# The opening of an attention and mixture-of-experts kernel: scores after two heads' maxima instead of four

## Chip, cores and metric

The kernel runs on one core of a Trainium2 chip. The metric is the device time of one execution in microseconds (us); the time of a kernel is the median of its runs. Engines are TensorE (PE in the profile; PEld are its weight loads), VectorE (DVE), ScalarE (ACT), GpSimd (POOL) and SyncE (SP), which here only issues transfers. A name with a q (SPq, ACTq) is the engine's sequencer, where transfers are issued.

## What is computed

```python
# 8 batches x 8 heads, 576 positions, head dimension 64
scores = q @ k.T / 8;  cum = cumsum(max(s, 0))
scores = where(causal, -1e9, scores + minimum(cum_k - cum_q, 0))
attn = exp(scores - rowmax);  x = attn / attn.sum() @ v
# then, for the 4608 rows of x (512 wide): a group of 4, an expert of 4 in it,
# out = group weight * expert weight * relu(x @ w1) @ w2
```

The change touches the attention stage only, which fills the first 420 us or so.

## The kernel before

**Work on one head.** There are 64 heads in 32 pairs; heads 2p and 2p + 1 form pair p. For each head TensorE makes the scores twice. The first time (the "maxima", `rowmax`, tiles `pm`) the queries stand on the rows: six matmuls of 64 to 448 columns, in one fp32r term, and VectorE reduces each with the mask to a maximum per query (tile `mx`, result in `mc`). The maxima are transposed on TensorE (`pmt`), split on VectorE into a high and a low row (`th`, `tl`), and two small transfers put these rows into rows 66 and 67 of the operand tile `WA`. That is the shift. The second time (`scores`, tiles `ps`) the keys stand on the rows: twelve matmuls, six from `WA` (68 rows: head dimension, two rows of cumulative sums, two of shift) and six from `WB` (the low parts). ScalarE takes the exponential into `pt` or `pu`, GpSimd zeroes what lies above the diagonal (an affine select, the "mask"), and `av` multiplies with the values in `VT`: 14 matmul records on TensorE, seven in the program. Then the result is normalised, transposed to rows and stored, and every fourth pair the router takes over a batch.

**Operands of a pair.** `load_raw(p)` brings q and k of a pair into one of three tiles `r`. `split` makes the high part on ScalarE (`hl`) and the low part by a subtraction (VectorE for pair 0, GpSimd for the others; its queue is "G"). `load_a` and `load_b` move the parts with transfers into `WA` (four tiles) and `WB` (five); in the first four pairs `place` lets ScalarE write some of them directly. `cumh` holds the cumulative sums in SBUF, `cumd` a copy in DRAM. `ones(i)` sets the constant rows of a `WA` tile.

**Steps.** The main loop runs over steps. Step n makes the scores of head n, the AV matmuls of head n - 1 and the maxima of head n + 4 (`LEAD = 4`). Steps -4 to -1 only make the maxima of heads 0 to 3; so the scores of head 0 come after four heads' maxima. Within a step a string gives the order by hand: `A3` is the fourth maximum matmul, `B0` the first unit of scores, `C2` the third AV matmul; a lower- or upper-case letter alone takes one waiting piece of work from a queue, such as `a` (maximum on VectorE), `b` (exponential), `e` (mask), `v` (AV result), `T`, `t` and `D` (transpose, split and transfer of shift rows), `G` (a low part), `S` (a split), and `R` a step of the router. Every engine keeps that order: TensorE, VectorE, ScalarE and GpSimd through step 62, and SyncE through step 0; after that SyncE's order is chosen by the scheduler.

The router object is made before the first step; its constants are set on GpSimd, and `operands()` makes six more on VectorE, one piece at each `R`, in steps 2 and 3.

Of the kernel before, what the change touches and what calls it, by code (L numbers as in the profile page):

```python
# [8 lines left out]
F32 = mybir.dt.float32  # L9
# [105 lines left out]
def attention(tc, qk, v, s, wr, xs, st):  # L115
# [3 lines left out]
    with ExitStack() as ctx:  # L119
# [57 lines left out]

        def load_a(p, placed=False):
            w = WA[p % NA]
            hl = hls[p].bitcast(F32)  # L180
            for h in range(2):
                if h or not placed:
                    nc.sync.dma_start(w[0:64, :, h, QO:].bitcast(F32), hl[h * 64:h * 64 + 64, 0:2])
                n = 2 * p + h
                nc.sync.dma_start(w[64:66, KA, h, QO:].bitcast(F32), (cumh if p < 4 else cumd)[n:n + 1].bitcast(F32))

        def load_b(p, placed=False):
            w = WB[p % NBB].bitcast(F32)
            hl = hls.pop(p).bitcast(F32)
            for h in range(2):  # L190

                hr = slice(h * 64, h * 64 + 64)
                b = slice(1 if placed and h else 0, 2)
                if h or not placed:
                    nc.sync.dma_start(w[0:64, QA, h], hl[hr, 1])
                nc.sync.dma_start(w[64:128, b, h], hl[hr, 0::2][:, b])
# [4 lines left out]
        def rowmax(n):  # L201
# [11 lines left out]
            def item(j, q0, rows, w, c0, cw):  # L213

                if n < LEAD and (j + c0) % 2:
# [10 lines left out]
                def most():  # L226
# [4 lines left out]
                    if h and c0:  # L231
                        push("T", p, lambda: shift_rows(p))
# [5 lines left out]
        def shift_rows(p):  # L238
            need("a", 2 * p + 1)
            i = p % NA  # L240
            pt = small(f"pmt{p}")
            nc.tensor.transpose(pt[:10, :P], mc[p % 2], ident)
            push("t", p, lambda: shifts(p, i, pt))

        def shifts(p, i, pt):
            th = sm.tile([10, P], F32R, name=f"th{p}", tag="th", bufs=1)
            tl = sm.tile([10, P], F32R, name=f"tl{p}", tag="tl", bufs=1)
            nc.vector.tensor_scalar(out=th, in0=pt[:10, :P], scalar1=-1.0, scalar2=None, op0=ALU.mult)
            nc.vector.scalar_tensor_tensor(out=tl, in0=pt[:10, :P], scalar=-1.0, in1=th.bitcast(F32), op0=ALU.mult,
                                           op1=ALU.subtract)  # L250
# [5 lines left out]
            push("D", p, send)  # L256
# [222 lines left out]
        def ones(i):  # L479
            for a in (QA, KA):  # L480
                nc.gpsimd.memset(WA[i][64:66 if a == QA else 68, a].bitcast(F32).rearrange("p h q -> p (h q)"), 1.0)

        nc.vector.tensor_scalar(out=r1, in0=s0, scalar1=0.0, scalar2=8.0, op0=ALU.max, op1=ALU.mult)

# [3 lines left out]
        ones(0)  # L488
# [14 lines left out]
        ones(1)  # L503
        ones(2)
        place(0, 0)
        split(0, 0)
        split(0, 1)
        load_a(0, True)
        split(1, 0)
        split(1, 1)  # L510
        place(0, 1)
        place(0, 2)
        place(1, 0)
        load_a(1, True)
        load_b(0, True)
        rt = Router(tc, ac, late, end, small, ring, wr_f, wr_sb, xs, st)
        place(1, 1)
        place(1, 2)
        place(2, 0)
        split(2, 0)  # L520
        split(2, 1)
        place(2, 1)
        place(2, 2)
        ones(3)
        for t in VT:
            nc.gpsimd.memset(t[:, 0:NB, 2], 1.0)


        pre = {-2: [(load_a, 2, True)],
               -1: [(load_b, 1, True), (load_v, 0), (load_raw, 3), (load_raw, 4)],  # L530
               0: [(place, 3, 0), (split, 3, 0), (split, 3, 1), (load_a, 3, True), (place, 3, 1), (place, 3, 2), (load_v, 1)],
               1: [(split, 4, 0), (split, 4, 1), (load_b, 2, True), (load_raw, 5)]}
# [7 lines left out]
        FIRST = [o.split() for i, o in enumerate((  # L540
# [4 lines left out]
        LAST = FIRST  # L545
        ENDS = ["W O o K X L M Q".split(), []]
        ORDER0 = "B0 b e A0 a T t B1 b D A1 a B2 b e A2 a B3 b e e A3 a B4 b e A4 a A5 a".split()
        for step in range(-LEAD, NH + 5):
            m, a = step + LEAD, step - 1
            A = rowmax(m) if m < NH else []  # L550
            Bq, C = [], []
            if 0 <= step < NH:
                need("T", step // 2)
                need("t", step // 2)
                need("D", step // 2)
# [12 lines left out]
            if step >= 2 and step // 2 + 4 < NP:  # L568
                push("S", step // 2 + 4, lambda p=step // 2 + 4, part=step % 2: split(p, part, True))
            named = {"A": A, "B": Bq, "C": C}  # L570
            order = FIRST if step < 3 else ORDERS if step < NH - 1 else LAST if step < NH + 2 else ENDS
            for part in order[step % 2] if step > 0 else ORDER0:
                if part[0] in named:
# [9 lines left out]
            for f, *args in pre.get(step, ()):  # L583
                f(*args)
            if step == -1:
                nc.sync.dma_start(cumd, cumh.bitcast(F32))
                rt.queue.append(rt.operands())
# [6 lines left out]
            if step % 2 == 0 and 0 < step and step // 2 + 5 < NP:  # L594
                need("S", step // 2 + 3)
                need("G", step // 2 + 3)
                load_raw(step // 2 + 5)
            if step % 2 == 1 and 0 < step < NH:
                for f, lead in ((load_a, 4), (load_b, 3), (load_v, 1)):
                    if step // 2 + lead < NP and (f != load_v or step > 1):  # L600
                        need("S", step // 2 + lead)
                        if f == load_b:
                            need("G", step // 2 + lead)
# [1105 lines left out]
```

## Time and profile before

| | us |
|---|---|
| median of 3 runs | 877.28 (876.32 to 877.72) |
| profiled execution | 876.57 |
| its span, from the first to the last instruction | 874.8 |
| TensorE busy | 840.2 |
| VectorE, ScalarE, GpSimd busy | 718.9, 615.7, 603.2 |

The span is one execution seen by the profiler; its own time holds 1.77 us more. Busy times are sums over the span, and matmuls are pipelined, so that a busy TensorE is not one at its peak.

### The profile page before, as it was taken

The numbers are of one execution on the slowest core, as the hardware profiler recorded it, in microseconds if no ns is written. First come the engines' busy times: TensorE is split into PE (matmuls) and PEld (weight loads), VectorE is DVE, ScalarE is ACT, GpSimd is POOL, SyncE is SP. The second block draws the span as 40 slices with busy tenths as digits, with TensorE's granted clock in tenths as the row PEclk, the third lists the DMA queues.
The fourth block names the chain that finished last, engine by engine and source line by source line (L and its number), as shares of the span: only waits on it lengthen the run. The fifth ranks groups of instructions, "written<-read, shape, count | busy, mean of one in ns | idle before, by whom it ended". The sixth has DMA issues, their size and how long they took to land. (4 is left out here: it accounts for less than half of the span.)

```text
span 874.8 us, 17801 instructions
## 1 busy us (share of the span) xinstructions
PE 840.2 (96%) x5601; PEld 774.2 (89%) x5601; DVE 718.9 (82%) x1975; ACT 615.7 (70%) x1397; POOL 603.2 (69%) x746
## 2 busy tenths in 40 slices
PE   4999999999999999998799999999999999999997
PEld 2788888888888888886689999999999999999996
DVE  7567787787878788787468799999999999999972
ACT  5668777787868777776656656776677767777760
POOL 9767677676877768545657956776777777777660
PEclk9999999999999999999899999999999999999999
DMA  6999898897979898723546655555656565666620
GB/s 189 256 246 253 233 243 225 218 244 195 251 208 241 224 238 209 180 63 121 173 137 216 219 175 202 203 175 187 228 202 195 182 220 198 235 211 223 218 94 26
DMA packets 81877, 174.06 MB, mean 199 GB/s; under 512 B 9676, under 2 KB 45132, under 8 KB 73584
## 3 DMA queue, kind: packets, MB, share of 16 engines
q1 hardware_dynamic: 71664, 152.93, 59.6%
q0 software_dynamic: 7488, 18.89, 5.8%
q10 hardware_dynamic: 2624, 1.03, 0.5%
q8 instruction: 46, 0.75, 0.3%
q14 instruction: 55, 0.45, 0.2%
HBM read 108.97 MB, written 19.69 MB: 147 GB/s over the span
## 5 line engine op out<-in xcount | busy, mean ns | idle before, releaser
L1016 POOL TENSOR_TENSOR wl<-raw,wh 128x512 fp32r<-128x512 f32 x163 | 209.7, 1299 | 82.4 <-ACT wh L1013 58.6
L1013 ACT CAST wh<-raw 128x512 fp32r<-128x512 f32 x256 | 153.9, 616 | 1.8 <-issue 1.8
L228 DVE CUSTOM_DVE_ANT_0 mx<-pm,mask 128x192 bf16<-128x192 f32 (+4 forms) x320 | 127.2, 418 | 31.4 <-PE pm L220 28.7
L1133 PE MATMUL ph<-xh,wh 128*128 128x256 f32 (+13 forms) x512 | 140.3, 300 | 1.8 <-DVE hl L1140 1.8
L220 PE MATMUL pm<-WA 66*128 66x288 f32 (+4 forms) x384 | 123.8, 355 | 15.3 <-DMA WA<-ch 9.5
L276 PE MATMUL ps<-WA 68*128 68x320 f32 (+4 forms) x384 | 135.9, 358 | 2.0 <-DMA WA<-tl 1.9
L1133 PE MATMUL ph<-xl,wh 128*128 128x256 f32 (+13 forms) x512 | 137.8, 301 | 0.0
L316 PE MATMUL po<-pt,VT 128*128 128x256 f32 (+3 forms) x512 | 119.4, 352 | 1.3 <-issue 1.0
L1212 PE MATMUL py<-hh,wh 128*128 128x256 f32 (+13 forms) x448 | 112.9, 302 | 0.0
L1212 PE MATMUL py<-hl,wh 128*128 128x256 f32 (+13 forms) x448 | 112.4, 301 | 0.0
L1139 ACT ACTIVATE hh<-ph 128x256 fp32r<-128x256 f32 (+13 forms) x128 | 53.3, 418 | 83.8 <-PE ph L1133 82.9
L278 PE MATMUL ps<-WB 128*128 128x320 f32 (+4 forms) x384 | 110.7, 301 | 0.0
L1265 DVE STREAM_TRANSPOSE yr<-yT 32x384 f32<-32x384 f32 (+1 forms) x208 | 104.6, 503 | 4.5 <-ACT yT L1209 0.4
L316 PE MATMUL po<-pu,VT 128*128 128x320 f32 (+1 forms) x384 | 105.5, 383 | 1.3 <-POOL pu L295 1.3
L1103 DVE STREAM_TRANSPOSE xt<-xg 32x256 f32<-32x256 f32 (+1 forms) x208 | 102.4, 492 | 2.7
L316 PEld LDWEIGHTS po<-pt,VT 128*128 128x128 f32 x512 | 88.2, 192 | 13.9 <-issue 1.5
L1133 PEld LDWEIGHTS ph<-xh,wh 128*128 128x128 f32 x512 | 95.9, 190 | 2.1 <-DVE hl L1140 1.9
L1133 PEld LDWEIGHTS ph<-xl,wh 128*128 128x128 f32 x512 | 95.2, 190 | 0.2
L162 POOL TENSOR_TENSOR WB<-r,hl 64x576 fp32r<-64x576 f32 x62 | 88.0, 1420 | 6.1 <-DMA WB<-hl 1.8
L1133 PE MATMUL ph<-xh,wl 128*128 128x256 f32 (+13 forms) x512 | 92.0, 299 | 0.0
L220 PEld LDWEIGHTS pm<-WA 66*128 66x128 f32 (+1 forms) x384 | 69.2, 193 | 25.1 <-DVE mc L228 9.8
L380 POOL TENSOR_TENSOR xTl<-xT,xTh 128x512 fp32r<-128x512 f32 x30 | 38.2, 1272 | 76.0 <-ACT xTh L376 55.4
(249 smaller groups left out, 2007.3 us busy)
## 6 DMA issues: line engine op xcount, KB each, us to landing
raw<-in_w_dram SPq DMA_DIRECT2D x64, 1024.0 KB
r<-in_qk_dram SPq DMA_DIRECT2D x32, 576.0 KB
WA<-hl SPq DMA_DIRECT2D x60, 288.0 KB
WB<-hl SPq DMA_DIRECT2D x60, 288.0 KB
VT<-in_v_dram SPq DMA_DIRECT2D x32, 384.0 KB
WB<-hl SPq DMA_DIRECT2D x64, 144.0 KB
xs<-xr SPq DMA_DIRECT2D x15, 512.0 KB
WA<-cumd SPq DMA_DIRECT2D x56, 4.5 KB
```

What stands on the lines that cost most here:

```text
L162: (nc.vector if p < 1 else nc.gpsimd).tensor_tensor(out=hl[:, 2] if part else WB[p % NBB][0:64, KA, h], in0=r[hr, part], in1=hl[hr, part]. ...
L220: nc.tensor.matmul(ps[:rows, :cw], WA[i][0:66, QA, h, QO + q0:QO + q0 + rows], WA[i][0:66, KA, h, QO + c0:QO + c0 + cw], start=True, stop= ...
L228: nc.vector.tensor_tensor_reduce(out=tmp[:rows, :cw], in0=ps[:rows, :cw], in1=mk[:rows], scale=1.0, scalar=-3.0e38 if c0 == 0 else mo, op0 ...
L276: nc.tensor.matmul(ps[:rows, o:o + w], WA[i][0:68, KA, h, QO + k0:QO + k0 + rows], WA[i][0:68, QA, h, QO + q0:QO + q0 + w], start=True, st ...
L278: nc.tensor.matmul(ps[:rows, o:o + w], WB[p % NBB][:, KA, h, k0:k0 + rows], WB[p % NBB][:, QA, h, q0:q0 + w], start=False, stop=True)
L316: nc.tensor.matmul(po[0][:, qa - base:qb - base], VT[p % NVT].rearrange("p t a d -> p (t a d)")[:, (3 * t + 1 + h) * 64:][:, 0:P], x[:, c: ...
L1013: self.casts.append(nc.scalar.copy(h[:, j], raw[:, j]))
L1016: self.low = lows[self.u, i, j] = nc.gpsimd.tensor_tensor(out=l[:, j], in0=raw[:, j], in1=h[:, j].bitcast(F32), op=ALU.subtract)
L1103: V.transpose(dst[:, 0:n, :, j], src[:, 0:n, :, i])
L1133: self.product = nc.tensor.matmul(pss[f][:, :cap], w[f // 4][:, c, (f % 4) * P:(f % 4 + 1) * P], x[:, c, :cap], start=(c == 0 and w is sel ...
L1212: self.product = nc.tensor.matmul(pss[c][:, :cap], w[2 + f // 4][:, f % 4, c * P:(c + 1) * P], x[:, f, :cap], start=(f == 0 and w is self. ...
L1265: V.transpose(dst[:, 0:n, :, i], src[:, 0:n, :, j])
```

## The change

The steps start at -1. In step -1 the maxima of heads 0 and 1 are made (the new token `N` takes the next maximum matmul, of whatever head is next), and step 0 makes the scores of head 0. The lead grows from two heads back to four in steps 1 to 6, which have eight `N` each instead of six. Eight order strings (`OPEN`) give the order of steps -1 to 6, the transfers' issue on SyncE among it: places, splits, low parts, loads and `ones` are tokens in them. Pair 0 sends the shift rows of each head by itself, `th` from ScalarE's queue and `tl` from SyncE's. ScalarE places head 1 of pair 0 in `WA` (a transfer did it). All low parts are made on GpSimd. The router object is made at the end of step 4; four of the six operand operations on VectorE are replaced by two iotas, the other two move to GpSimd. From pair 4 on one transfer brings the cumulative sums of both heads. From step 7 on the order strings are as before; the low parts of a pair are made two steps later than before.

```diff
-        def split(p, part, later=False):
-            if part == 0:
+        def split(p, part):
+            if p not in hls:
                 hls[p] = raw.tile([P, 3, S], F32R, name=f"hl{p}", tag="hl", bufs=3)
...
-                (nc.vector if p < 1 else nc.gpsimd).tensor_tensor(
-                    out=hl[:, 2] if part else WB[p % NBB][0:64, KA, h], in0=r[hr, part],
-                    in1=hl[hr, part].bitcast(F32), op=ALU.subtract)
+                nc.gpsimd.tensor_tensor(out=hl[:, 2] if part else WB[p % NBB][0:64, KA, h], in0=r[hr, part],
+                                        in1=hl[hr, part].bitcast(F32), op=ALU.subtract)
             for h in range(1 if part else 2):
-                if later:
-                    push("G", p, lambda h=h: low(h))
-                else:
-                    low(h)
+                push("G", p, lambda h=h: low(h))
...
             nc.scalar.copy(*((WA[p][0:64, :, 0, QO:], raws[p][0:64]) if part == 0 else
+                             (WA[p][0:64, :, 1, QO:], raws[p][64:128]) if part == 3 else
                              (WB[p][0:64, QA, 0], raws[p][0:64, 1]) if part == 1 else
...
-                if n < LEAD and (j + c0) % 2:
+                if n < 2 and (j + c0) % 2:
                     ps = ps_s.tile([P, 512], F32, name=f"pm{n}_{j}_{c0}", tag="ps")
...
-                    if h and c0:
-                        push("T", p, lambda: shift_rows(p))
+                    if c0 and (h or p == 0):
+                        push("T", p - (1 - h) / 2, lambda: shift_rows(p, h))
...
                 for r, t in ((66, th), (67, tl)):
-                    nc.scalar.dma_start(WA[i][r:r + 1, QA].bitcast(F32).rearrange("o h q -> o (h q)"), t.bitcast(F32))
+                    d = WA[i][r:r + 1, QA].bitcast(F32)
+                    e = nc.sync if r == 67 and p == 0 else nc.scalar
+                    e.dma_start((d if p else d[:, h:h + 1]).rearrange("o h q -> o (h q)"), t[:n].bitcast(F32))
...
+        ones(0, nc.vector)
         nc.vector.tensor_scalar(out=r1, in0=s0, scalar1=0.0, scalar2=8.0, op0=ALU.max, op1=ALU.mult)
...
+        OPEN = [o.split() for o in (
+            "c0 p00 p03 s01 G s00 c1 G G b00 c2 s11 s10 h1 p01 p10 w0 "
+            "N N N N N N N tt a v0 p02 t D N N N N b01 s21 s20 N G",
+            "N tt a t D r3 B0 b B1 b N a e h2 p11 B2 b N a e p12 B3 b e N a G B4 p20 b e N a G N a",
+            "B0 b N a C0 B1 b N a e C1 v v b10 b11 B2 b N a C2 r4 B3 b e N a C3 w1 o3 N a e B4 N b N tt a t D e C4 C5 "
+            "N a C6 v v v1 G c3 cd",
+            "C0 N a s31 C1 v v N a C2 B0 b s30 N a B1 b e C3 N a p30 B2 b e h3 N a C4 C5 B3 b N a e C6 v v e N a B4 b "
+            "N a p21 p22 b20 b21 r5",
+            "C0 B2 N a B0 N tt v e C1 B1 a t B3 v D N a Y b N a v a e b C2 b N a s41 e C3 N a e b e C4 v s40 N a Z B4 a "
+            "G N a C5 b C6 a p31 p32 a4 v2",
+            "B0 v b a N B2 v C0 e G a N a B3 C1 N a B1 N a C2 b e G C3 v N a s51 C4 B4 b v e a N a N tt a W e t C5 e D C6 b "
+            "N a s50 b30 b31 r6 a5 rt",
...
-        for step in range(-LEAD, NH + 5):
+        for step in range(-1, NH + 5):
             m, a = step + LEAD, step - 1
-            A = rowmax(m) if m < NH else []
+            A = rowmax(m) if len(OPEN) - 2 < step and m < NH else []
...
-            if step == 0:
+            if step == len(OPEN) - 2:
                 manual.close()
                 manual.enter_context(tc.manual_schedule(engines={ENG.PE, ENG.DVE, ENG.Activation, ENG.Pool}))
...
-        n1 = iota("n1", [[S, B], [P, NB]], base=1, cm=1, dt=I32)
-        self.part = ac.tile([P, 2, B, NB], F32, name="part")
-        ni = ac.tile([P, B, NB], I32, name="ni")
-        self.n1, self.ni, self.uf, self.onesf = n1, ni, uf, onesf
+        self.part = (iota("part0", [[S // 64, B], [P // 64, NB]]), iota("part1", [[0, B], [0, NB]], base=1, cm=1))
+        nc.gpsimd.tensor_copy(self.ub, uf)
+        nc.gpsimd.memset(self.ob, 1.0)
```

In the strings, `c` loads cumulative sums, `p` places (pair, part), `s` splits, `b` loads `WB` (pair, head), `h` loads head 1 of a pair into `WA`, `a` with a digit both heads, `r` a raw tile, `v` with a digit a tile of values, `w` and `o` set constants, `tt` makes the transpose of the maxima at once, `rt` the router object and `cd` writes `cumd`.

## Rows read from the trace of the kernel before

**Rows 1.** The page: busy time of each engine, share of the span, instructions.
```profile
PE 840.2 (96%) x5601; PEld 774.2 (89%) x5601; DVE 718.9 (82%) x1975; ACT 615.7 (70%) x1397; POOL 603.2 (69%) x746
```
**Rows 2.** Windows: stretch, length, busy PE, PEld, DVE, ACT, POOL; clock, DMA share, GB/s.
```profile
22.69:28.42 5.73, 5.53 (x22) 4.83 (x23) 2.82 (x13) 2.49 (x6) 3.36 (x8) 1.00 0.93 309
28.42:33.07 4.65, 4.65 (x15) 4.00 (x16) 1.35 (x8) 4.45 (x10) 3.23 (x3) 1.00 0.73 221
33.07:35.87 2.80, 2.80 (x20) 2.41 (x18) 1.62 (x6) 1.14 (x2) 2.66 (x7) 1.00 0.92 255
35.87:43.91 8.04, 7.34 (x40) 5.40 (x38) 7.37 (x21) 6.20 (x15) 6.19 (x8) 1.00 1.00 240
43.91:51.75 7.84, 5.78 (x29) 4.93 (x27) 5.76 (x18) 3.87 (x9) 4.42 (x7) 0.78 0.88 241
51.75:57.55 5.80, 5.80 (x37) 5.11 (x36) 3.88 (x13) 4.18 (x11) 4.44 (x6) 1.00 1.06 263
57.55:62.69 5.14, 5.14 (x37) 4.65 (x35) 4.08 (x18) 4.54 (x13) 2.57 (x5) 1.00 0.91 258
62.69:68.46 5.77, 5.77 (x38) 5.09 (x36) 3.88 (x13) 4.63 (x12) 5.57 (x9) 1.00 0.94 210
...
46.38:51.75 5.37, 5.37 (x26) 4.74 (x26) 3.33 (x14) 2.86 (x7) 2.27 (x4) 0.68 0.95 271
```
**Rows 3.** Timeline of the start: start us, length, engine, line, operation [idle before].
```profile
3.84 0.48 DVE L483 TENSOR_SCALAR cl<-cl 64x576 f32<-64x576 f32 x1 [3.84 <-DMA cl<-in_s_dram]
7.48 0.77 SPq L185 DMA_DIRECT2D WA<-ch  x1
9.45 0.95 PE L220 MATMUL pm<-WA 66*128 66x288 f32 x3 [9.45 <-DMA WA<-ch]
9.93 0.76 DVE L162 TENSOR_TENSOR hl<-r,hl 128x576 fp32r<-128x576 f32 x1
10.60 0.45 DVE L228 CUSTOM_DVE_ANT_0 mx<-pm,mask 128x288 bf16<-128x288 f32 x1
12.75 0.51 DVE L228 CUSTOM_DVE_ANT_0 mx<-pm,mask,mc 128x288 bf16<-128x288 f32 x1
15.91 0.38 PE L242 MATMUL pmt<-ident,mc 128*10 128x128 f32 x1 [0.21 <-DVE mc L228]
16.64 0.28 DVE L249 SCALAR_TENSOR_TENSOR tl<-pmt,th 10x128 fp32r<-10x128 f32 x1
16.64 1.62 ACTq L254 DMA_DIRECT2D WA<-th  x1
18.35 0.74 ACTq L254 DMA_DIRECT2D WA<-tl  x1
22.72 0.55 PE L276 MATMUL ps<-WA 68*128 68x256 f32 x1 [1.88 <-DMA WA<-tl]
```
**Rows 4.** Timeline: first and last of the router's six operations, then TensorE's wait.
```profile
37.63 1.42 DVE L699 CAST ub<-uf 128x128 bf16<-128x128 f32 x1
...
44.47 1.43 DVE L707 CAST part<-ni 128x40 f32<-128x40 int32 x1
...
46.38 0.36 PE L220 MATMUL pm<-WA 66*128 66x192 f32 x1 [2.06 <-DVE mc L228]
```
**Rows 5.** Timeline: ScalarE, GpSimd and a SyncE issue; last, a window of GpSimd's constants.
```profile
6.62 1.15 ACT L174 CAST WA<-r 64x1152 fp32r<-64x1152 f32 x1 [4.04 <-DMA r<-in_qk_dram]
7.68 2.39 ACT L158 CAST hl<-r 128x576 fp32r<-128x576 f32 x4
11.47 2.88 POOL L162 TENSOR_TENSOR WB<-r,hl 64x576 fp32r<-64x576 f32 x2
12.54 0.67 SPq L196 DMA_DIRECT2D WB<-hl  x1
...
15.78:17.60 1.82, 1.75 (x13) 1.00 0.40 108
```
**Rows 6.** Windows of steps 4 to 6, masks on GpSimd alone: length, busy, count.
```profile
51.75:68.46 16.71, 4.50 (x12) 1.00 0.97 243
```

More of the change, by code (lines that the diff above doesn't have):

```diff
@@ L176, in place, with load_h @@
                              (WB[p][64:128, KA, 1], raws[p][64:128, 0])))
-        def load_a(p, placed=False):
-            w = WA[p % NA]
-            hl = hls[p].bitcast(F32)
[L181 to L196, printed above, removed]
+        def load_h(p, h):
+            nc.sync.dma_start(WA[p % NA][0:64, :, h, QO:].bitcast(F32), hls[p].bitcast(F32)[h * 64:h * 64 + 64, 0:2])
@@ new lines, in load_c, with load_a, load_b @@
+        def load_c(p):
+            if p < 4:
+                for h in range(2):
+                    n = 2 * p + h
+                    nc.sync.dma_start(WA[p][64:66, KA, h, QO:].bitcast(F32), cumh[n:n + 1].bitcast(F32))
+            else:
+                nc.sync.dma_start(WA[p % NA][64:66, KA, :, QO:].bitcast(F32), cumd[2 * p:2 * p + 2].rearrange("h a s -> a h s"))
+        def load_a(p):
+            load_h(p, 0)
+            load_h(p, 1)
+            load_c(p)
+        def load_b(p, h, placed=False):
+            need("G", p)
+            w = WB[p % NBB].bitcast(F32)
+            hl = hls[p].bitcast(F32)
+            hr = slice(h * 64, h * 64 + 64)
+            b = slice(1 if placed and h else 0, 2)
+            if h or not placed:
+                nc.sync.dma_start(w[0:64, QA, h], hl[hr, 1])
+            nc.sync.dma_start(w[64:128, b, h], hl[hr, 0::2][:, b])
@@ L502, in attention, with router, most, turn @@
         make_identity(nc, ident)
-        ones(1)
         ones(2)
[L505 to L532, printed above, removed]
+        route_by = []
+        def router():
+            route_by.append(Router(tc, ac, late, end, small, ring, wr_f, wr_sb, xs, st))
+            route_by[0].queue.append(route_by[0].operands())
+        maxima, begun = [], [0]
+        def most():
+            if not maxima:
+                maxima.extend(rowmax(begun[0]))
+                begun[0] += 1
+            maxima.pop(0)()
+        def turn():
+            while not fifo["T"]:
+                pop("a")
+            pop("T")
+        acts = {"N": most, "tt": turn, "rt": router, "cd": lambda: nc.sync.dma_start(cumd, cumh.bitcast(F32))}
+        for n in range(10):
+            acts.update({f"o{n}": lambda n=n: ones(n), f"w{n}": lambda n=n: nc.gpsimd.memset(VT[n][:, 0:NB, 2], 1.0),
+                         f"r{n}": lambda n=n: load_raw(n), f"v{n}": lambda n=n: load_v(n), f"a{n}": lambda n=n: load_a(n),
+                         f"h{n}": lambda n=n: load_h(n, 1), f"c{n}": lambda n=n: load_c(n)})
+            for i in range(4):
+                acts.update({f"s{n}{i}": lambda n=n, i=i: split(n, i), f"p{n}{i}": lambda n=n, i=i: place(n, i),
+                             f"b{n}{i}": lambda n=n, i=i: load_b(n, i, n < 4)})
         vals, sums, pts = {}, {}, {}
@@ L539, in attention @@
             "e C4 v A1 Z B4 a R A5 C5 b C6 t a a"))]
[L540 removed]
+        LAST = [o.split() for o in (
             "B4 b e A1 a R B0 b e B1 b C0 A0 a R J T t C1 v v D A2 a R W C2 B2 b e O o Q A3 a R B3 b e e A4 a "
@@ L567, in attention @@
                 C = av(a, pts.pop(a), vals[p], sums[p])
-            if step >= 2 and step // 2 + 4 < NP:
-                push("S", step // 2 + 4, lambda p=step // 2 + 4, part=step % 2: split(p, part, True))
+            if step >= len(OPEN) - 2 and step // 2 + 4 < NP:
+                push("S", step // 2 + 4, lambda p=step // 2 + 4, part=step % 2: split(p, part))
             named = {"A": A, "B": Bq, "C": C}
-            order = FIRST if step < 3 else ORDERS if step < NH - 1 else LAST if step < NH + 2 else ENDS
-            for part in order[step % 2] if step > 0 else ORDER0:
-                if part[0] in named:
+            order = (OPEN[step + 1] if step + 1 < len(OPEN) else
+                     (ORDERS if step < NH - 1 else LAST if step < NH + 2 else ENDS)[step % 2])
+            for part in order:
+                if part in acts:
+                    acts[part]()
+                elif part[0] in named:
                     for f in named[part[0]][int(part[1]):int(part[1]) + 1]:
@@ L582, in attention @@
                     pop(part)
[L583 to L587, printed above, removed]
+            rt = route_by[0] if route_by else None
             if step == 62:
```

73 lines of the change are left out of this document (32 added, 41 removed), and 6 rows, old and new, of tables (FIRST, LAST, OPEN).

## Prediction

> **What bounds the kernel now.** I read the page first: TensorE is busy for 96% of the span, ahead of every other engine [rows 1]. A time saved anywhere is therefore kept only if TensorE's own line of work gets shorter or starts earlier. Then the windows, one for each step (the boundaries are the first score matmul of a step, or its first AV matmul where that comes first). Steps 4, 5 and 6 last 5.80, 5.14 and 5.77 us with TensorE busy throughout, 5.47 us in the mean of a pair (steps 4 and 5): the settled pace. Step 0 starts only at 22.69, and steps 1, 2 and 3 last 7.45, 8.04 and 7.84 us [rows 2]. So the opening loses time in two ways: a late start, and three long steps. From step 7 on, TensorE, VectorE and ScalarE execute the same instructions in the same order in both kernels (read off the order strings), so what is gained by then is kept.
>
> Then the timeline of the start. The first maximum matmul waits until 9.45 for the cumulative sums, which were issued at 7.48. VectorE is free for the first maximum at about 10.0 but still makes a low part from 9.93, and starts at 10.60; the last maximum of head 0 starts at 12.75 and takes 0.51. The transpose of the maxima runs at 15.91 because it waits for both heads; the low row `tl` is made at 16.64, issued only at 18.35, and TensorE waits for its landing until 22.72 [rows 3]. The scores are late by a transfer, not by the maxima of heads 2 and 3, which fill the wait.
>
> Third, the waits: the six operand operations of the router sit on VectorE between 37.63 and 45.9, in steps 2 and 3, and at 46.38 TensorE has waited 2.06 us for a maximum behind them [rows 4]. The stretch after it ran at a granted clock of 0.68, 26 matmuls in 5.37 us, 0.207 each, where step 4 has 37 in 5.80, 0.157 each [rows 2].
>
> **The change, part by part.** *Start of step 0.* Head 0's low part leaves VectorE, so its six maxima run from about 10.05 instead of 10.60 and end at 10.05 + 2.66 (12.75 + 0.51 - 10.60) = 12.7. From the transpose to the end of `tl` took 15.91 to 16.92, so `tl` is ready at 13.8 [rows 3]. On ScalarE the placing of two heads (1.15 each), four splits (2.39), one more place and two half ones (0.58 each) end at 6.62 + 7.0 = 13.6, in time for `th`. SyncE must first issue the loads put ahead of it: the first needs the low part that now runs on GpSimd (split done at 9.5, plus 1.44, so 11.0), then five issues of 0.67: 14.3 [rows 5]. The landing is the unknown: from issue to use, `ch` took 9.45 - 7.48 = 1.97 and `tl` 22.69 - 18.35 = 4.34 [rows 3]. The head's other transfers are just ahead of it on the queue, so I take 3.0, near the middle: step 0 starts at 17.3 (16.3 to 18.6), **-5.4**. The memsets of `ones(0)` on VectorE cost nothing, because VectorE waits for the data until 3.84; without that cover they would delay the cumulative sums by their length.
>
> [...]
>
> *Step 0* has the same matmuls as before: 5.73, no change. *Step 1* has two more maximum matmuls at the slow pace of the window from 28.42 (15 in 4.65, 0.31 each): +0.6. It also ends with a transpose that follows the maxima at once. Such a wait lies between 0.21 (the transpose at 15.91) and one maximum, 0.51 [rows 3]; 0.35 here, with one matmul between: **+0.95**.
>
> *Steps 2 to 6* each have two more maximum matmuls, 2 x 0.157 = 0.31, since two heads of lead (12 items) are made up in them and step 1. Their AV matmuls stand in more separate pieces; for that I take 0.3 a step (0 to 0.6), two matmuls' worth. Transposes that follow their maximum at once: 0.5 in steps 3 and 6, 0.35 in step 4.
>
> *Step 2* also needs the rows of heads 2 and 3, now made at the end of step 1. From the transpose, `tl` is ready after 1.0, `th` 0.28 earlier; both are issued by ScalarE, 0.74 each, then 1.97 to land: 0.73 + 0.74 + 1.97 = 3.4. TensorE has the transpose (0.38) and 15 matmuls of 0.157 ahead of these scores, 2.7: a wait of 0.7 (0 to 3.1, with 4.34 for the landing). ScalarE has its splits (2 x 0.60), a place (1.15) and two half places (1.16) on top of about 3.9 of a settled step (4.5 less a split) [rows 2, 5], 7.4 in all against 6.8, which I charge with 0.4. So step 2 is 5.47 + 0.31 + 0.3 + 0.7 + 0.4 = 7.2 where it was 8.04: **-0.85**. The router's operations are no longer on VectorE, so *step 3* is 5.47 + 0.31 + 0.3 + 0.5 = 6.6 where it was 7.84: **-1.25**. *Steps 4, 5, 6*: +0.95, +0.6, +1.1, **+2.65** together.
>
> Sum: -5.4 + 0.95 - 0.85 - 1.25 + 2.65 = **-3.9 us**. The profiled execution took 876.57 (span 874.8 and 1.77 around it), so 872.7; the median of the runs is 877.28, 0.71 above it, so the forecast is **873.4**.
>
> *Costed at nothing.* GpSimd: in steps 4 to 7 it has 13 low parts (1.44 each), 17 masks (4.50 / 12 = 0.375) and the router's constants (1.82 and about 0.6 more), 27.5 us [rows 5, 6] against 24.4 of step time, so it falls behind by 3. A mask is read a step later, which covers it; without that cover it costs 3. Transfers: raw tiles are loaded later, but one 288 KB transfer falls away and the windows moved 240 to 270 GB/s [rows 2]. The single `cumd` load for each later pair and the relaxed order of raw loads lie behind a busy TensorE.
>
> **The rivals.** *All of it hidden* (chance 0.20): no wait for rows in step 2, none at transposes, no cost of the pieces. Then -5.4 + 0.6 - 2.26 - 2.06 + 0.93 = -8.2: 869.1. For it: in the settled steps no transpose waits. Against: these orders put it right behind its maximum.
>
> *Late rows* (0.13): each shift row lands 4.34 after issue. Step 0 starts at 18.6 (+1.35) and step 2 waits 3.1 (+2.4): -0.15, 877.1. For it: the only landing of such a row that the trace shows; against: that window had the DMA share at 0.93 right after, and less is in flight now.
>
> *GpSimd becomes the bound* (0.08): masks come late in steps 5 to 8, 3 us back: -0.9, 876.4.
>
> *Slower: the slow pace lasts longer* (0.11). [...]
>
> **How the numbers follow.** Forecast 0.48 (its own range 871.0 to 875.5), hidden 0.20, late 0.13, GpSimd 0.08, slower 0.11. What can be told from no change is 0.2%, 1.75 us. Faster: 0.48 + 0.20 = 0.68; same: 0.13 + 0.08 = 0.21; slower 0.11. The range runs from 869.0, which cuts about half of the hidden case, to 878.5, which cuts the slower one.
>
> **What would show it.** First score matmul near 17.3, its wait put down to `tl`. No router operation on VectorE near 40, and no 2 us wait at a maximum. Step 2's first score waits under 1.5 us for `tl`. Steps 3 to 6 of 5.7 to 6.9 us with TensorE over 90% busy. The forecast is wrong if step 0 starts after 19, if the matmuls are still 0.25 apart after 32 us, or if ScalarE or GpSimd is what TensorE waits for in steps 2 to 6.

## The result and the profile after

The changed kernel takes 889.32 us, median of four runs (888.43 to 893.84), against 877.5 for the kernel before: a ratio of 1.0138, 95% interval 1.0094 to 1.0182. It is slower by 12 us, where 4 us less were forecast (873.4, range 869.0 to 878.5). The profiled execution is the longest of the four (893.84, span 892.1). It is 17.3 us longer than the profiled one before, and 12.9 of them are there when step 10 starts; that part, the opening, is what I read. Steps 10 to 19 take 59.6 us in both; the other 4.4 us come later in this one execution, and no run was made on them.

The page's first line answers [rows 1]:

```profile
PE 845.3 (95%) x5602; PEld 776.1 (87%) x5602; DVE 717.7 (80%) x1970; ACT 618.4 (69%) x1398; POOL 606.2 (68%) x750
```

Nothing is to be seen there: the same work, on the same engines. The windows of the steps (0, 1, 2, 3, 4, 5, 6, then 7 from its first AV matmul, then 8 and 9; columns as in [rows 2]) show the loss:

```profile
18.58:23.27 4.69, 4.69 (x17) 4.16 (x18) 1.42 (x7) 3.67 (x7) 1.06 (x4) 1.00 0.87 209
23.27:32.79 9.52, 9.21 (x36) 7.48 (x36) 4.73 (x22) 3.60 (x9) 8.02 (x11) 1.00 0.54 157
32.79:39.91 7.12, 6.02 (x36) 4.92 (x35) 2.91 (x13) 5.69 (x12) 0.72 (x3) 1.00 0.39 82
39.91:47.26 7.35, 6.33 (x36) 4.88 (x36) 5.65 (x24) 5.69 (x13) 4.75 (x8) 1.00 0.56 168
47.26:55.52 8.26, 6.29 (x37) 5.15 (x36) 5.21 (x20) 5.31 (x12) 6.65 (x20) 1.00 0.75 190
55.52:62.59 7.07, 6.64 (x38) 5.24 (x39) 4.17 (x19) 6.61 (x16) 5.46 (x10) 1.00 0.64 172
62.59:78.05 15.46, 6.54 (x37) 4.99 (x36) 6.43 (x20) 5.45 (x13) 7.50 (x10) 0.86 0.99 217
78.05:86.28 8.23, 8.23 (x37) 7.52 (x37) 3.52 (x14) 4.38 (x11) 4.27 (x8) 0.64 1.05 232
86.28:97.40 11.12, 11.12 (x71) 9.84 (x70) 8.10 (x29) 9.30 (x24) 9.71 (x13) 1.00 1.00 265
```

Step 6 starts at 62.59 where it was 62.69 before [rows 2], so by then the early start has been given back, but nothing is lost. Then step 6 takes 15.46 instead of 5.77. Look at the column before the last: the DMA share is 0.39 to 0.75 from step 1 to step 5, where the kernel before had 0.73 to 1.06, and from step 6 on it is 1.0. Two windows from the start, to step 6 and to step 10, first of the kernel before:

```profile
0.00:62.69 62.69, 46.38 (x211) 37.22 (x211) 42.95 (x149) 38.77 (x79) 48.31 (x97) 0.97 0.84 232
0.00:84.52 84.52, 68.21 (x349) 56.72 (x349) 58.91 (x209) 57.06 (x125) 64.55 (x121) 0.98 0.86 237
```

and of the changed one:

```profile
0.00:62.59 62.59, 44.82 (x209) 35.26 (x210) 36.00 (x138) 40.08 (x78) 41.23 (x93) 1.00 0.60 165
0.00:97.40 97.40, 70.71 (x349) 57.61 (x350) 54.05 (x201) 59.21 (x126) 62.70 (x122) 0.95 0.75 191
```

Length times share is the transfer time used: 72.7 us to step 10 before, 73.1 after. It is nearly the same transfer time (for somewhat fewer bytes: 237 GB/s over 84.52 us is 20.0 MB, 191 over 97.40 is 18.6), done by 84.52 in one and by 97.40 in the other: what differs is the time in which the DMA engines stood, 11.8 against 24.3 us. At step 6 the changed kernel has used 37.6 us of it, the kernel before 52.7.

Why they stood is in the timeline (raw loads, low parts on GpSimd, and what TensorE and ScalarE waited for):

```profile
14.54 0.87 SPq L260 DMA_DIRECT2D WA<-tl  x1
18.58 0.55 PE L282 MATMUL ps<-WA 68*128 68x256 f32 x1 [1.94 <-DMA WA<-tl]
24.84 1.41 POOL L162 TENSOR_TENSOR WB<-r,hl 64x576 fp32r<-64x576 f32 x1
26.28 0.33 SPq L151 DMA_DIRECT2D r<-in_qk_dram  x1
35.74 0.36 PE L282 MATMUL ps<-WA 68*128 68x256 f32 x1 [0.18 <-DMA WA<-tl]
40.14 2.89 POOL L162 TENSOR_TENSOR WB<-r,hl 64x576 fp32r<-64x576 f32 x2
43.06 0.34 SPq L151 DMA_DIRECT2D r<-in_qk_dram  x1
51.69 1.40 POOL L162 TENSOR_TENSOR WB<-r,hl 64x576 fp32r<-64x576 f32 x1
53.20 0.54 SPq L151 DMA_DIRECT2D r<-in_qk_dram  x1
62.39 1.40 POOL L162 TENSOR_TENSOR WB<-r,hl 64x576 fp32r<-64x576 f32 x1
63.81 0.35 SPq L151 DMA_DIRECT2D r<-in_qk_dram  x1
70.96 1.28 SPq L202 DMA_DIRECT2D VT<-in_v_dram  x2
73.71 0.67 ACT L158 CAST hl<-r 128x576 fp32r<-128x576 f32 x1 [4.35 <-DMA WB<-hl]
78.05 1.19 PE L322 MATMUL po<-pt,VT 128*128 128x256 f32 x2 [7.84 <-DMA VT<-in_v_dram]
```

Each raw load (pairs 4, 5, 6, 7) goes out 0.02 to 0.11 us after the end of the last low part of the pair three before, which held its tile. The low parts stand late in GpSimd's order, and SyncE keeps the written order through step 6, so all that is written behind a raw load waits with it, the values of pair 3 (70.96) too. In the kernel before the same four loads went out earlier (the first row is pair 3's load and pair 4's):

```profile
20.26 1.58 SPq L151 DMA_DIRECT2D r<-in_qk_dram  x2
...
30.19 0.33 SPq L151 DMA_DIRECT2D r<-in_qk_dram  x1
36.13 0.85 SPq L151 DMA_DIRECT2D r<-in_qk_dram  x1
47.83 0.94 SPq L151 DMA_DIRECT2D r<-in_qk_dram  x1
```

The four go out some 5, 13, 17 and 16 us later than there. In the stretch after the wait of 7.84 us (78.05 to 86.28) the granted clock reads 0.64, and 37 matmuls take 8.23, where 38 took 5.77 at 1.00 [rows 2].

### The profile page after: what moved, and what is told of

Same layout as the page of the kernel before. It is cut to its first block, busy times and chain, and to the rows that moved or that the text cites. A ratio compares the mean times of both kernels' runs of the same rounds, so it can differ in the third digit from the quotient of the medians.

```text
span 892.1 us, 17668 instructions
## 1 busy us (share of the span) xinstructions
PE 845.3 (95%) x5602; PEld 776.1 (87%) x5602; DVE 717.7 (80%) x1970; ACT 618.4 (69%) x1398; POOL 606.2 (68%) x750
## 3 DMA queue, kind: packets, MB, share of 16 engines
q10 hardware_dynamic: 2604, 1.02, 0.4%
## 5 line engine op out<-in xcount | busy, mean ns | idle before, releaser
L322 PE MATMUL po<-pt,VT 128*128 128x256 f32 (+3 forms) x512 | 121.8, 354 | 12.5 <-DMA VT<-in_v_dram 9.3
L162 POOL TENSOR_TENSOR WB<-r,hl 64x576 fp32r<-64x576 f32 x64 | 91.1, 1424 | 2.6
L301 POOL TENSOR_SCALAR_AFFINE_SELECT pt<-pt 128x128 f32<-128x128 f32 (+2 forms) x192 | 64.9, 350 | 38.3 <-ACT pt L292 34.7
```

The lines of the kernel that those rows point to most:

```text
L162: nc.gpsimd.tensor_tensor(out=hl[:, 2] if part else WB[p % NBB][0:64, KA, h], in0=r[hr, part], in1=hl[hr, part].bitcast(F32), op=ALU.subtract)
L322: nc.tensor.matmul(po[0][:, qa - base:qb - base], VT[p % NVT].rearrange("p t a d -> p (t a d)")[:, (3 * t + 1 + h) * 64:][:, 0:P], x[:, c: ...
```

## The experiments

Three theories come up first in the expectations; later ones are named where they come. **S**: the opening is bound by its transfers, and the change lets the DMA engines stand. **Q**: the value loads alone are late, because they are written last in SyncE's order. **R**: the engines' own order, the maxima caught up in steps 1 to 6 above all, is too long. All ratios are to the kernel before, run on the same chip.

**Values early.** The value loads of pairs 2 and 3 are written earlier in the strings.

```diff
-            "N a p21 p22 b20 b21 r5",
+            "N a p21 p22 b20 b21 v2 r5",
...
-            "N a s50 b30 b31 r6 a5 rt",
+            "N a s50 b30 b31 r6 a5 v3 rt",
...
```

> The changed kernel with two value loads moved forward in SyncE's hand-written order: the second pair's behind the WB loads of step 2, the third's to the end of step 4. Theory Q (the loads of values stand behind transfers that wait for later work, and TensorE waits 1.42 us and 7.84 us for them at 55.52 and 78.05): both waits go, and with them most of the 2.7 us of slow matmuls behind the second: 889.3 - 9.3 - 2.7, about 877. Theory S (transfers run dry from 30 to 50 us because raw tiles come free late, 110 GB/s where the kernel before moved about 228, and what is left over falls due at once from 60 us on): only the thing waited for changes, since the raw tile of pair 7 landed at 73.7 and holds ScalarE until then: 884 to 887.

889.27 us, 1.0148 (1.0128 to 1.0169). The wait for values is gone and nothing is gained:

```profile
73.28 0.67 ACT L158 CAST hl<-r 128x576 fp32r<-128x576 f32 x1 [3.94 <-DMA WB<-hl]
74.34 0.41 PE L282 MATMUL ps<-WA 68*128 68x320 f32 x1 [1.51 <-ACT pu L292]
83.93 0.67 ACT L158 CAST hl<-r 128x576 fp32r<-128x576 f32 x1 [4.15 <-DMA WB<-hl]
85.25 0.41 PE L282 MATMUL ps<-WA 68*128 68x320 f32 x1 [1.96 <-ACT pt L292]
```

ScalarE stops at a split until the loads that read the tile `hl` have run, and TensorE pays for it. Q falls: the longest wait named only the load that happened to come last. S had the change of waits right, but its time (884 to 887) is missed too.

**SyncE's order left to the scheduler** from step 1 on, as before the change.

```diff
-            if step == len(OPEN) - 2:
+            if step == 0:
                 manual.close()
```

> The changed kernel, but SyncE keeps the hand-written order only through step 0, as in the kernel before; from step 1 on the scheduler places its transfers. Theory Q: the scheduler issues the values as soon as their tile is free (it did so before, at 57.37), the two waits go: about 877. Theory S: raw tiles come free no earlier, 884 to 887.

886.73 us, 1.0135 (1.0101 to 1.0168), spread from 882.92 to 890.21. This is S's number. Its profiled execution is the fastest of the four, the change's the slowest: there step 10 starts at 89.14 instead of 97.40, but the time isn't told from the change's.

**Four raw tiles** (and four `WB` tiles instead of five), raw loads of pairs 4 to 7 one place earlier.

```diff
-        NA, NBB, NVT = 4, 5, 2
+        NA, NBB, NVT = 4, 4, 2
-            raws[p] = raw.tile([P, 2, S], F32, name=f"r{p}", tag="r", bufs=3)
+            raws[p] = raw.tile([P, 2, S], F32, name=f"r{p}", tag="r", bufs=4)
...
```

> The changed kernel with a fourth raw tile (paid for with one of the five WB tiles) and the raw loads of pairs 4 to 7 one place earlier in SyncE's order; the values stay last. Theory S: the DMA share between 30 and 50 us rises from 0.43 to over 0.6, the wait for values at step 7 falls from 7.84 to under 3: 881 to 884. Theory Q: the values still stand last behind the same waiting transfers, 7 us or more of waiting: 887 to 890.

888.2 us, 1.0134 (1.0111 to 1.0157). The time is Q's, the wait is S's: at step 7 TensorE waits 1.98 us for values instead of 7.84, but the DMA share from 30 to 50 us is 0.44 where S wanted over 0.6. Step 10 starts at 90.16 in the profile, and 3.9 us of that lead are given back right behind it (19.45 us to the transpose of step 12, 15.58 in the change). The kernel also has one `WB` tile less to the end, so the run doesn't show what a raw tile alone is worth.

**Low parts early.** The strings are rewritten so that a pair's low parts, splits, places and loads come about one step earlier; two of the eight show the kind of edit.

```diff
-            "N N N N N N N tt a v0 p02 t D N N N N b01 s21 s20 N G",
+            "N N N N N N N tt a v0 p02 t D N N N N b01 s21 s20 N G G G",
-            "N tt a t D r3 B0 b B1 b N a e h2 p11 B2 b N a e p12 B3 b e N a G B4 p20 b e N a G N a",
+            "N tt a t D r3 b10 b11 h2 B0 b B1 b N a e p11 B2 b N a e p12 B3 b e N a G B4 p20 b e N a G N a r4",
```

> The changed kernel with the opening's order strings rewritten so that the low parts, the splits, the places, the operand loads and the raw loads of each pair come about one step earlier than in the change (pair 1's low parts in step -1, pair 2's by step 1, pair 3's in step 2, and so on); nothing is added or removed. Theory S (the opening is bound by its transfers, and the change starves the DMA engines between 10 and 55 us because raw tiles come free late): the transfer time left idle before step 10 falls from 24.6 us to about 13, step 10 starts by 85 instead of 97.4, and the time is 873 to 879. Theory R (the loss is made on the engines' own order, in steps 1 to 4, whatever the transfers do): idle transfer time falls but step 10 stays after 92 and the time is 884 or more. If the order only moves the waits to VectorE or ScalarE, the waits at TensorE name those engines and the time is 880 to 886.

888.45 us, 1.0106 (1.0074 to 1.0139). Step 10 starts at 91.82, 5.6 earlier in the profile, and the DMA engines stand for 17 us (a share of 0.81 over 91.82) instead of 24. The direction is S's, the size isn't: S expected 873 to 879 and step 10 by 85. R's time (884 or more) came, and its mark for step 10 (after 92) is missed by 0.2.

**Fewer loads in the changed kernel.**

```diff
-            "G N a C5 b C6 a p31 p32 a4 v2",
+            "G N a C5 b C6 a p31 p32 a4",
-            "b a r8 b50 b51")]
+            "b a r8")]
-                if p - 1 < NP:
+                if p - 1 < NP and p - 1 != 6:
```

> The changed kernel without the loads of the low-part operands of pairs 5 and 6 and without the load of the values of pair 2: 2.16 MB less, all issued between steps 4 and 9; those heads compute with what the tiles held before. 2.16 MB at the 250 GB/s of the busy windows is 8.6 us of transfer work. Theory S: the debt of transfers at 60 to 90 us is smaller by about 8 us, so step 10 starts at 89 to 91 and the time is 880 to 883. Theory L (only the value loads that TensorE is seen to wait for matter; of these one is dropped, the wait of 1.42): 887 to 888. Theory R (engines' order): 888 to 889, with no change of step 10.

893.26 us, 1.0170 (1.0139 to 1.0201): no gain at all, against S, and above what any theory expected (880 to 889). Its timeline:

```profile
70.58 1.32 SPq L202 DMA_DIRECT2D VT<-in_v_dram  x2
77.06 1.19 PE L322 MATMUL po<-pt,VT 128*128 128x256 f32 x2 [7.54 <-DMA VT<-in_v_dram]
```

Most of what I left out goes out after the values of pair 3, which still leave at 70.58. So the bound of the changed kernel isn't the sum of the bytes; it is when they can be issued. S must be split: **C**, a chain (late low part, late raw tile, late loads behind it), and **T**, the transfers as a whole, once they are issued in time.

**Both links of the chain eased**: low parts early, SyncE's order left to the scheduler (the two edits above together).

> The kernel with the opening's low parts, splits, places and loads one step earlier, and besides SyncE's order left to the scheduler from step 1 on (as in the kernel before) instead of by hand through step 6. Theory C (a chain: a pair's low parts are made late, so its raw tile comes free late, so the next raw load, and in SyncE's hand order all that stands behind it, is issued late, and the transfer time lost so is never made up): both links of the chain are eased, step 10 starts by 87 to 89 instead of 91.8 and the time is 880 to 884. Theory T (the transfers bind whatever their order is, as soon as they are started early): transfer time idle before step 10 is no smaller than with the early low parts alone, step 10 at 91 to 92, time 887 to 889.

884.51 us, 1.0083 (1.0060 to 1.0106), step 10 at 90.26. That is 4.8 us below the change (in another round; the intervals of the two ratios just overlap). Both numbers lie between the theories, nearer to C's (880 to 884, step 10 by 87 to 89) than to T's. Two long waits are left at TensorE: 2.54 us for `tl` at 50.72, and 2.01 at 60.25 for an exponential, while ScalarE stands for 4.60 around its two issues of shift rows.

**The same with fewer loads** (2.16 MB, as above).

> The same as the run with early low parts and SyncE's order left to the scheduler, without the loads of the low-part operands of pairs 5 and 6 and of the values of pair 2 (2.16 MB; those heads compute with what the tiles held). In the changed kernel itself this omission gave nothing. Theory C with theory T behind it (once the chain is eased the transfers themselves bind, as they do in the kernel before, where the omission gave 4 us): 4 us or more below its twin with all loads, step 10 at 84 or before. If something else binds (ScalarE or VectorE in the opening's order): within 1 us of the twin.

881.62 us, 1.0048 (1.0033 to 1.0063), step 10 at 86.01: 2.9 us below its twin (the intervals just touch), 4.3 in the profile at step 10. The expectation wanted 4 us and step 10 at 84. Of the twin's two long waits the one for `tl` is gone and the other is 1.02. What gave nothing in the changed kernel gives about 3 us here, which fits T standing behind C.

**The router's part alone on the kernel before**, to see what the 2.06 us wait of [rows 4] was worth.

```diff
-        n1 = iota("n1", [[S, B], [P, NB]], base=1, cm=1, dt=I32)
-        self.part = ac.tile([P, 2, B, NB], F32, name="part")
...
+        self.part = (iota("part0", [[S // 64, B], [P // 64, NB]]), iota("part1", [[0, B], [0, NB]], base=1, cm=1))
+        nc.gpsimd.tensor_copy(self.ub, uf)
+        nc.gpsimd.memset(self.ob, 1.0)
```

> The kernel before with the router's part of the change alone: four operand operations of VectorE replaced by two iotas, two moved to GpSimd. If the 2.06 us wait at 46.38 and the slow stretch behind it come from these operations: 877.5 - 2.1 to 877.5 - 3.4, so 874.1 to 875.4. If TensorE would wait there for something else: 877.5.

877.49 us, 1.0008 (0.9988 to 1.0028): nothing that can be measured. The wait behind the router's operations is gone, and another stands ten us later:

```profile
52.02 0.75 ACTq L254 DMA_DIRECT2D WA<-th  x1
55.89 0.73 ACTq L254 DMA_DIRECT2D WA<-tl  x1
56.67 0.38 ACT L324 ACTIVATE sums<-po 64x256 f32<-64x256 f32 x1 [5.86 <-DMA WA<-th]
57.14 1.19 PE L316 MATMUL po<-pt,VT 128*128 128x256 f32 x2 [4.13 <-issue]
```

**The router's part and fewer loads.**

```diff
-                    if step // 2 + lead < NP and (f != load_v or step > 1):
+                    if step // 2 + lead < NP and (f != load_v or step > 3) and (f != load_b or step // 2 + lead not in (5, 6)):
```

> The kernel before with the router's part of the change alone (as in the run with the router alone), and without the loads of the low-part operands of pairs 5 and 6 and of the values of pair 2: those heads compute with what the tiles held. Theory S (the router's wait was hidden behind the transfers, which bind the opening of the kernel before as well): the wait of 4.13 for the values is gone and the missing gain shows: 872 to 875. If the transfers bind nothing there: 877 to 878, as with the router's part alone.

873.61 us, 0.9940 (0.9913 to 0.9966). The wait is gone and the gain shows: once the router's part is out of the way, the transfers bind the opening of the kernel before. (A load left out takes away its bytes and also every wait on it. The run further below that only moves the values of pairs 2 and 3 earlier gains nothing, which speaks for the bytes.) This kernel and the one with early low parts and fewer loads leave out the same loads, both have the router's part, and in neither does TensorE wait over 0.6 us for a transfer from step 1 to step 10; they differ by 8.0 us in the medians and by 6.4 in the profiles at step 10. There the difference ends: steps 10 to 19 take 59.56 and 59.72 us, though the later loads of cumulative sums and low parts aren't placed alike either. Steps 4, 5 and 6, first on the kernel before (this one), then on the changed one:

```profile
46.88:53.46 6.58, 6.58 (x40) 5.82 (x39) 4.43 (x16) 4.54 (x11) 5.35 (x9) 1.00 0.87 220
53.46:57.79 4.33, 4.33 (x32) 3.92 (x31) 3.53 (x14) 4.19 (x12) 2.55 (x4) 1.00 0.65 165
57.79:64.38 6.59, 6.59 (x41) 5.82 (x40) 4.43 (x16) 4.98 (x12) 5.59 (x9) 1.00 0.52 141
```

```profile
47.46:55.99 8.53, 7.22 (x41) 5.78 (x41) 5.53 (x22) 4.28 (x10) 8.04 (x22) 1.00 0.85 220
55.99:61.90 5.91, 5.48 (x34) 4.40 (x34) 3.76 (x16) 5.18 (x14) 5.25 (x8) 1.00 0.46 151
61.90:70.41 8.51, 7.43 (x42) 6.11 (x41) 5.62 (x20) 5.11 (x12) 4.12 (x7) 1.00 0.39 93
```

22.95 us against 17.50: 2.6 more of TensorE's own time (20.13 busy against 17.50) and 2.8 in which it stands. The start of step 0 is 2.1 us earlier, steps 0 to 9 are 8.5 longer, 5.45 of it here. This is R's part.

**Waits of the hand order.** On the kernel with both links eased, two transposes stand later and one exponential earlier.

```diff
-            "v2 C0 B2 N a B0 N tt v e C1 B1 a t B3 v D N a Y b N a v a e b C2 b N a s51 e G C3 N a e b e C4 v s50 N a Z B4 a "
+            "v2 C0 B2 N a B0 N v e C1 B1 tt a t B3 v D N a Y b N a v a e b C2 b N a s51 e G C3 N a e b e C4 v s50 N a Z B4 a "
...
-            "B0 v b a N B2 v C0 e G a N a B3 C1 N a B1 N a C2 b e G C3 v N a s61 C4 B4 b v e a N a N tt a W e t C5 e D C6 b "
+            "B0 v b a N B2 v C0 e G a N a B3 C1 N a B1 N a C2 b e G C3 v N a s61 C4 B4 b v e a N a N tt a W e t C5 e b D C6 "
...
-            "B0 v b a N N tt B2 v C0 a t e G a N a B3 D C1 N a B1 N a C2 b e G C3 v N a C4 B4 b v e a N a W e N C5 e C6 S "
+            "B0 v b a N N B2 v C0 tt a t e G a N a B3 D C1 N a B1 N a C2 b e G C3 v N a C4 B4 b v e a N a W e N C5 e C6 S "
```

> The kernel with early low parts and SyncE's order left to the scheduler, with three places of the hand order changed: in steps 3 and 6 the transpose of the maxima stands a few tokens later, so that TensorE needn't wait for VectorE's last maximum (0.79 at 42.3 and 1.03 at 68.2 us there), and at the end of step 4 ScalarE takes the last exponential before it issues the shift rows (TensorE waits 2.01 for that exponential at 60.25). Theory R (what is left of the loss once the transfers are eased is the opening's own order: the maxima caught up in steps 1 to 6 and the waits around them): the three waits go, step 7 starts 2.5 to 3.5 us earlier, 881 to 882. Theory T (the transfers bind there anyway): other waits, for operands, take their place and the time stays at 884 to 885.

884.55 us, 1.0093 (1.0066 to 1.0120). This is T's number. The three waits are gone and step 10 starts 1.1 us earlier in the profile, but the time is that of its twin: 2.12 us for `tl` at 50.71 stay, and waits of 0.45 to 0.70 for ScalarE's exponentials are new. With all loads in place, what is taken out of the order is not kept; R's waits aren't the bound by themselves. The same edit on the kernel with fewer loads, where it could show, was not run.

**Transfers into the gap.** On the kernel with the router's part, the values of pairs 0 and 1 go out at about 8 and 15 us; in the second kernel ScalarE also places pair 4.

```diff
             for h in range(2):
+                if p == 0 and h:
+                    load_v(0)
                 if h or not placed:
...
         load_b(0, True)
+        load_v(1)
...
-               1: [(split, 4, 0), (split, 4, 1), (load_b, 2, True), (load_raw, 5)]}
+               1: [(split, 4, 0), (split, 4, 1), (place, 4, 0), (place, 4, 1), (place, 4, 2), (load_b, 2, True), (load_raw, 5)]}
...
```

> The kernel before with the router's part of the change, and with the values of pairs 0 and 1 loaded in the gaps of the transfers at 8 to 10 and 16 to 18 us (they were issued at 19.6 and 32.6); nothing of the opening's maxima changes. The two loads are 0.59 MB, 2.4 us at the 250 GB/s of the busy windows, moved from a full stretch into an idle one. If the transfers bind the opening: step 10 some 2 us earlier than in the kernel before and the time 873.5 to 876. If TensorE and the engines bind: 877 to 878.

> The run before it in this list, and besides ScalarE places three operand blocks of pair 4 (1.15 and twice 0.58 us in step 2) which three transfers of 0.59 MB in all brought. If the transfers bind: another 2 us, 871 to 874. If ScalarE's 2.3 us in step 2 delay the exponentials instead: 876 to 880, with TensorE waiting for ScalarE at 36 to 44 us.

878.44 us, 1.0007 (0.9988 to 1.0025), and 881.75 us, 1.0049 (1.0032 to 1.0065). Both miss what was expected if the transfers bind (873.5 to 876, and 871 to 874), and the second is slower than its rival's range (876 to 880) as well. One new wait in each:

```profile
13.71 0.95 PE L222 MATMUL pm<-WA 66*128 66x288 f32 x3 [1.75 <-DMA WA<-hl]
```

```profile
42.78 0.74 PE L278 MATMUL ps<-WA 68*128 68x448 f32 x1 [2.45 <-ACT pt L288]
```

In the first the bulk load is ahead of the operand of head 1's maxima, and step 0 starts later (23.85); what was moved into the gap cost what it saved. In the second ScalarE's 2.3 us delay the exponentials, the mechanism that the rival named.

**One load earlier, or ScalarE freed.** On the kernel with the router's part: the values of pairs 2 and 3, or of all pairs, one step earlier; or the shift rows issued by SyncE; or both.

```diff
+               2: [(load_v, 2)], 4: [(load_v, 3)]}
...
-                    nc.scalar.dma_start(WA[i][r:r + 1, QA].bitcast(F32).rearrange("o h q -> o (h q)"), t.bitcast(F32))
+                    (nc.scalar if p < 2 else nc.sync).dma_start(WA[i][r:r + 1, QA].bitcast(F32).rearrange("o h q -> o (h q)"), t.bitcast(F32))
```

> The kernel before with the router's part of the change, and the loads of the values of pairs 2 and 3 put one step earlier in the program, at the end of the step in which their tile comes free. Theory T (transfers bind the opening of the kernel before): the wait of 4.13 for the values goes, but the operand loads that were ahead land later, so another wait takes its place: 876 to 878. Theory V (that one load was merely late in the order, the transfers have room): the router's 2 to 4 us show, 872 to 875.

877.22 us, 1.0010 (0.9992 to 1.0029). The values now go out at 40.17, and TensorE still stands at the same matmul:

```profile
51.55 0.75 ACTq L254 DMA_DIRECT2D WA<-th  x1
55.29 0.72 ACTq L254 DMA_DIRECT2D WA<-tl  x1
56.06 0.38 ACT L324 ACTIVATE sums<-po 64x256 f32<-64x256 f32 x1 [6.81 <-DMA WB<-hl]
56.54 1.19 PE L316 MATMUL po<-pt,VT 128*128 128x256 f32 x2 [5.08 <-issue]
```

T's number. So it isn't the values: ScalarE stands between its two issues of shift rows, and the exponentials behind them are late.

> The same for the values of all pairs from 2 on: each is loaded one step earlier than in the kernel before. Theory T: as the run before it, 876 to 878, and nothing is gained after step 10, where no wait for values is seen. Theory V: 872 to 875, no better than moving the two early ones.

877.29 us, 1.0004 (0.9990 to 1.0019): as the run before it.

> The kernel before with the router's part of the change, and the shift rows of pairs 2 and on issued by SyncE instead of ScalarE. In the run with the router's part alone ScalarE stood for 5.86 us between two issues of shift rows (52.0 and 55.9) while the DMA engines were full, and TensorE then waited 4.13. [...] Theory T (the transfers as a whole bind the opening, whoever issues): another wait for an operand takes its place, 876 to 878.

875.59 us, 0.9992 (0.9969 to 1.0014). ScalarE's stop and the wait at 57 us are gone, and a wait for an operand stands 14 us later:

```profile
71.00 0.36 PE L276 MATMUL ps<-WA 68*128 68x256 f32 x1 [1.62 <-DMA WA<-tl]
```

It is the lowest median of a kernel with all loads and 0.41 below T's range, but it isn't told from the kernel before.

> The same, and the values of all pairs from 2 on loaded one step earlier. [...] Theory T: 876 to 878.

878.52 us, 1.0016 (0.9993 to 1.0038): T's number.

> The changed kernel with early low parts, SyncE's order left to the scheduler and the three order changes, and the shift rows of pairs 2 and on issued by SyncE. With ScalarE issuing them it stood for 4.60 us at 55 to 60 us. [...] Theory T: 884 to 886, the wait is for operands instead.

On the kernel of the order waits, with SyncE issuing the rows: 883.27 us, 1.0062 (1.0037 to 1.0088). ScalarE's stop is gone; the number is 0.73 below T's range, and isn't told from its twin's 884.55.

No version with all its loads beats the kernel before by more than can be measured.

## Why the prediction was wrong

**The step that failed** is in "Costed at nothing": "Transfers: raw tiles are loaded later, but one 288 KB transfer falls away and the windows moved 240 to 270 GB/s". It rests on the first sentence of the reading, that TensorE bounds the kernel. The page's 96% is a mean over the span; up to step 6 TensorE was busy for 46.38 of 62.69 us, and the windows of steps 2 to 6 in [rows 2] have the DMA share at 0.88 to 1.06. I read their GB/s as room to spare, where the share in the column beside it said that there was little. The router's part on the kernel before gave nothing with all loads (1.0008) and 0.9940 with 2.16 MB of them left out: the transfers were the bound behind TensorE's waits. "Raw tiles are loaded later" was then the cost itself: 5 to 17 us later each, 12.5 us more in which the DMA engines stood.

**How the 12 us come about**, by medians: late issue (low parts late, SyncE's written order) 4.8, which the two edits together win back (889.32 to 884.51); the other 7.0 lie between that kernel and the kernel before with the router's part (884.51 and 877.49), and with fewer loads in both the gap is 8.0. It is the order of the opening, of which 5.45 us show in steps 4 to 6. There the forecast had +2.65, and the kernel before needs 17.53 us for the same stretch, as the kernel with the router's part and fewer loads does. The maxima alone (tile `pm`, length of the stretch, then TensorE's time on them), before, then in the two kernels with fewer loads, the changed one last:

```profile
51.75:69.28 17.53, 5.86 (x19) 1.00 0.97 248
46.88:64.38 17.50, 5.84 (x19) 1.00 0.68 177
47.46:70.41 22.95, 8.47 (x25) 1.00 0.58 155
```

So TensorE's 2.6 us more are the six maxima caught up here, 0.44 each by the trace's lengths (the ends of matmuls are modelled), where the forecast put them at 0.157 each: a second term that was too small. Of the 2.8 in which TensorE stands, 2.4 are waits for VectorE's maxima (0.37 and 1.03) and for an exponential of ScalarE (1.02). What these waits are worth stays open: taking such waits away was tried only with all loads in place and gave nothing that could be measured.

**Step by step.** *Start of step 0*: 18.58, not 17.3. `tl` was issued at 14.54 (14.3 forecast) and landed after 4.04, not 3.0: the upper bound was right. In the kernel before `tl` took 4.34, issued by ScalarE; here SyncE issued it. *Step 0*: 4.69 for 5.73. *Step 1*: 9.52 for 8.4. *Step 2*: 7.12 for 7.2, by luck: the wait for the shift rows was 0.18 instead of 0.7, and TensorE stood for 0.92 at an AV matmul that the sum didn't have. *Step 3*: 7.35 for 6.6. *Steps 4, 5, 6*: 8.26, 7.07 and 15.46 for 6.75, 5.75 and 6.9. Up to step 6 the terms are off by 4.9 us together; 1.42 of them are a wait for values at the end of step 4, the rest are sizes. That wait, the 8.6 of step 6 and the 3.3 of steps 7 to 9 (19.35 where 16.06 were before) are of the kind that I had costed at nothing. Of the signs that I had named, three came or nearly so (the wait for `tl` before step 0, the router's, the short wait in step 2). The fourth did not: steps 3 to 6 took 7.07 to 15.46 us, with TensorE busy for 42 to 94%.

*The router*: its operations left VectorE and the 2.06 wait went, as said, but alone it is worth nothing that can be measured, since the transfers were the bound behind it. *"What is gained by then is kept"*: step 6 starts at the same time in both kernels, yet the changed one is 15 us of transfer time behind. A start time is no measure of what is in hand. *GpSimd*: I asked whether it has too much work (3 us); the place of its low parts in the order was the question.

*Rivals.* Late rows had the landing nearly right (4.34 for 4.04) and no more. The longer slow pace that "slower" took is an estimate of mine that no run shows. In the changed kernel the matmuls come 0.26 apart from 23.27 to 30.00 (26 in 6.73) and 0.19 apart from there to 32.79 (13 in 2.48 of busy time), where the kernel before still had 0.31 up to 33.07 [rows 2], and the granted clock reads 1.00 up to 62.59. A lower clock came later (0.64 from 78 to 86), behind a wait for a transfer that had already cost 7.84. No rival had the transfers as the bound, so "slower" got 0.11 for another reason, and the range ended 10.8 us short.

## What to carry to other kernels

Read the share of the DMA engines in each stage beside that of the engines, before naming a bound. Here it was 0.88 to 1.06 in the stages that the forecast took for TensorE's alone: the router's gain of 2 us was not kept there, and loads that left 5 to 17 us later were not made up. Where tiles rotate, follow the release of each tile to the issue of the next load, and the issue to all that stands behind it in the same written order. Price the work that a reordering moves by what it costs where it goes, and not at the settled pace (here 0.44 us a maximum against 0.157). And when a long wait is removed and nothing is gained, look for the next wait before looking for a mistake: here three edits each took a wait of 2 to 8 us away (7.84 for values, 2.06 behind the router, 4.13 at ScalarE's stop), and each time another of 1.5 to 4.1 us took its place.

## What the runs showed of the hardware

In two runs ScalarE stood around its two issues of 5 KB rows: 5.86 us with the router's part alone (issues at 52.02 and 55.89), with the DMA share at 1.05 from 50 to 57 us, and 6.81 us with the values of pairs 2 and 3 early (issues at 51.55 and 55.29), where the packets of queue q1 alone took 100.9% of the 16 DMA engines' time from 40 to 60 us. In the second case SyncE too issued nothing from 50.91 to 54.97. With the rows issued by SyncE (the router's part), ScalarE's longest wait from 47.5 to 62.4 us was 0.62, and SyncE took 0.76 to 0.86 for each row. The share alone doesn't tell these cases apart: in the kernel before, at 1.06 (53 to 55 us), ScalarE issued the same two rows at 54.34 and 55.18 and waited 0.72. What held the issue isn't shown.
